# Windowed attention with sinks and top-128 experts: the first K and Q loaded uncast in halves, turned by fp32 products, later loads held by marks

## The chip, the cores and the metric

The kernel runs on one core of a Trainium2 chip. The core has TensorE (PE, with its weight loads shown apart as PEld), VectorE (DVE), ScalarE (ACT), GpSimd (POOL) and SyncE (SP), which issues most of the loads and stores. The metric is the device time of one execution in microseconds, as the median of several. A profiled execution gives a trace in which every instruction has its start and its length.

## The reference

Attention for 4 batches of 8 heads over 768 tokens of 64 columns. A query sees the 128 keys up to itself and the first 4 keys, the sinks. The result, laid out as rows of 512, goes through a block that picks the 128 rows with the largest gate score in each batch and adds the gated output of two layers to them.

```python
scores = scale * np.matmul(q, k.transpose(0, 1, 3, 2))
keep = is_sink | in_window          # 4 sinks, or 0 <= query - key < 128
scores = np.where(keep, scores, -1000000000.0)
a = softmax(scores); out = np.matmul(a, v)
x = out.transpose(0, 2, 1, 3).reshape(B, S, H * D)
scores = x @ w_gate
for b in range(B):                  # the 128 rows with the largest scores
    xe = x[b, top_idx]
    ye = np.maximum(xe @ w1, 0.0) @ w2
    out[b, top_idx] = xe + sigmoid(scores[b, top_idx])[:, None] * ye
```

## The kernel before

The work is cut into 24 steps: 4 batches, two groups of 4 heads each (a pair of heads shares the 128 rows of a tile, so a group is called a pair of tiles, K and Q), and three pairs of 128-token blocks. The order of instructions on each engine is the order in which the program writes them. Each engine takes its own in order and waits by semaphores for what others make.

A pair (b, g) needs K and Q turned, with the 64 columns of a head on the partitions. `transposes` (L210) turns them on TensorE in two halves of 6 products each into a PSUM bank, and ACT (`L228`) and DVE (`L230`) copy the banks to `KT` and `QT`. The bf16 input of later pairs comes from `plain_qk` (L105), which loads fp32 through SP into a buffer of the pool `raw` (three buffers), and `cast_qk` (L113), which casts it on POOL in two pieces for each tensor. The first pair alone goes another way: `load_qk` (L96) lets the DMA cast, which POOL issues (L103), and both halves are turned one head at a time, 24 products for a tensor (L221).

`scores` (L235) makes the score products of one step (L246), adds the masks (L256) and the sinks' scores (L263, L267) and lets ACT take the exponentials (L274; L276 and L277 in the last step of a pair). `values` (L279) multiplies them with V in fp32 (L295), once for each half `t` of the heads; DVE divides (L298, L299) into the rows `x`. V stands in three tiles: `vb` as loaded, and `vlo` and `vhi`, in which one half of the partitions holds V again and four of the others the sinks' V. POOL copies V into them (`copy_half_values` L134, `copy_half_heads` L138). For the first pair the sinks' V is loaded into the first block (L145) and spread over the six blocks by POOL (L149). All other pairs get it from a table `vst`, which DVE spreads out of `vsk` in `stage_sinks` (L196 to L202) and SP copies into place (`load_sink_values`, L129).

The prologue (L152 to L194) writes out loads, clearings and masks; then `fill` (L545) keeps TensorE at work with products of a unit matrix whose results nobody reads, the first pair is turned, and the scores of step 0 are made (L553 to L561). The loop (L593 on) makes values of step n, scores of the step two ahead, and the turning of the next pair, and SP's loads are put where the table `PAIRS_AT` (L580) says. `sp_after` (L589) is a mark: SP copies one element of a finished row to a scrap tile, so that it waits for that step before it goes on to the loads behind it.

Of the kernel before, what the change touches and what calls it, by code (L numbers as in the profile page):

```python
# [9 lines left out]
FP32 = mybir.dt.float32  # L10
BF16 = mybir.dt.bfloat16
# [19 lines left out]
def kernel(  # L31
# [41 lines left out]
    vlo = [const([128, 4, NB, VW], FP32, f"vlo{i}") for i in range(2)]  # L73
    vhi = [const([128, 4, NB, VW], FP32, f"vhi{i}") for i in range(2)]
    vsk = mp.tile([NSINK * B, H, D], FP32, name="vsk", tag="junk")
    vst = const([NSINK * B, H, NB, VW], FP32, "vst")
    ksk = [const([128, 2, 64], BF16, f"ksk{i}") for i in range(2)]
    ident_f = const([128, 128], FP32, "ident_f")
# [12 lines left out]
    smark = const([1, 24], FP32, "smark")  # L91
    part = const([128, 2], FP32, "part")

    QKF, QK, KT, QT, PT, X, SCOL = {}, {}, {}, {}, {}, {}, {}

    def load_qk(b, g, ts=(0, 1)):  # L96
        for t in ts:
            name = ("kb", "qb")[t]
            dst = stg.tile([128, 2, CT, D], BF16, name=name, tag=name)
            QK[(b, g, t)] = dst  # L100
            src = (k, q)[t][b, 4 * g:4 * g + 4, :, :].rearrange("(l e) (p c) d -> (e p) l (c d)", e=2, c=CT)
            for l in range(2):
                POOL.dma_start(out=dst[:, l, :, :].rearrange("p c d -> p (c d)"), in_=src[:, l, :])  # L103

    def plain_qk(b, g, ts=(0, 1)):  # L105
        for t in ts:
            dst = raw.tile([128, 2, CT * D], FP32, name="raw", tag="raw")
            QKF[(b, g, t)] = dst
            src = (k, q)[t][b, 4 * g:4 * g + 4, :, :].rearrange("(l e) (p c) d -> (e p) l (c d)", e=2, c=CT)
            for l in range(2):  # L110
                SP.dma_start(out=dst[:, l, :], in_=src[:, l, :])

    def cast_qk(b, g, t):  # L113
        name = ("kb", "qb")[t]
        dst = stg.tile([128, CT, 2, D], BF16, name=name, tag=name)
        QK[(b, g, t)] = dst
        src = QKF[(b, g, t)][:, :, :].rearrange("p l (c d) -> p c l d", c=CT)
        for c in (0, CT // 2):
            POOL.tensor_copy(out=dst[:, c:c + CT // 2, :, :], in_=src[:, c:c + CT // 2, :, :])  # L119
# [23 lines left out]
    def first_sink_values():  # L143
        for dst, r in ((vlo, 64), (vhi, 0)):
            SP.dma_start(out=dst[0][r:r + NSINK, :, 0, 0:D], in_=v[0, 0:4, 0:NSINK, :].rearrange("h s d -> s h d"))  # L145

    def spread_first_sinks(c0, c1):
        for dst, r in ((vlo, 64), (vhi, 0)):
            POOL.tensor_copy(out=dst[0][r:r + NSINK, :, c0:c1, 0:D],  # L149
                             in_=dst[0][r:r + NSINK, :, 0:1, 0:D].to_broadcast((NSINK, 4, c1 - c0, D)))  # L150

    for b in range(B):  # L152
        ACTE.dma_start(out=vsk[NSINK * b:NSINK * b + NSINK, :, :], in_=v[b, :, 0:NSINK, :].rearrange("h s d -> s h d"))
    DVE.memset(ones_b[:], 1.0)
    ACTE.activation(out=warm[:], in_=ones_b[:], func=ACT.Exp)
    POOL.memset(ident_f[:], 0.0)
    POOL.affine_select(out=ident_f[:], in_=ident_f[:], compare_op=ALU.not_equal, fill=1.0, base=0,
                       pattern=[[-1, 128]], channel_multiplier=1)
    DVE.tensor_copy(out=ident_b[:], in_=ident_f[:])
    load_qk(0, 0)  # L160
    for dst, r in ((vlo, 64), (vhi, 0)):
        DVE.memset(dst[0][r:r + 64, :, :, :], 0.0)
        DVE.memset(dst[0][r:r + NSINK, :, :, D:VW], 1.0)
    load_v_block(0, 0, 0)
    load_v_block(0, 0, 1)
    first_sink_values()
    for c in range(2, NB):
        load_v_block(0, 0, c)
    plain_qk(0, 1)
    for h in (4, 6):  # L170
        load_v_heads(0, h)
# [13 lines left out]
    spread_first_sinks(1, 2)  # L185
# [7 lines left out]
    DVE.memset(vlo[1][64:128, :, :, :], 0.0)  # L193
    DVE.memset(vhi[1][0:64, :, :, :], 0.0)  # L194

    def stage_sinks():  # L196
        DVE.memset(vst[:, :, :, D:VW], 1.0)
        DVE.memset(vb[1][:, :, :, D:VW], 1.0)
        for g in range(2):
            DVE.tensor_copy(out=vst[:, 4 * g:4 * g + 4, :, 0:D],  # L200
                            in_=vsk[:, 4 * g:4 * g + 4, :].unsqueeze(2).to_broadcast((NSINK * B, 4, NB, D)))
        load_sink_values(0, 1)  # L202

    def late_consts2():
        for c in range(NB):
            DVE.memset(sel[:, c, 1:2], float(128 * c))
        DVE.tensor_copy(out=iota_b[:], in_=iota_i[:])
        DVE.tensor_copy(out=sel[:, :, 0:1], in_=tok_i[:, :].unsqueeze(1).to_broadcast((128, NB, 1)))

    def transposes(b, g, t, halves=(0, 1)):  # L210
        if 0 in halves:
            (KT, QT)[t][(b, g)] = tp.tile([128, 2, S], BF16, name=("KT", "QT")[t], tag=("KT", "QT")[t])
        src = QK[(b, g, t)]
        dst = (KT, QT)[t][(b, g)]
        for half in halves:
            trp = bank("w", [128, CT // 2, 128], BF16, "trp")
            for i in range(CT // 2):
                c = half * (CT // 2) + i
                if (b, g) == (0, 0):
                    for l in range(2):  # L220
                        PE.transpose(out=trp[64 * l:64 * l + 64, i, :], in_=src[:, l, c, :], identity=ident_b[:])  # L221
                else:
                    PE.transpose(out=trp[:, i, :], in_=src[:, c, :, :].rearrange("p l d -> p (l d)"),  # L223
                                 identity=ident_b[:])
            o = dst[:, :, :].rearrange("d e (p c) -> d e p c", c=CT)[:, :, :, half * (CT // 2):(half + 1) * (CT // 2)]
            i = trp[:, :, :].rearrange("d c (e p) -> d e p c", e=2)
            if (half if (b, g) == (0, 0) else 0) == t:
                ACTE.copy(out=o, in_=i)  # L228
            else:
                DVE.tensor_copy(out=o, in_=i)  # L230
# [314 lines left out]
    def fill(count):  # L545
        z = bank("xg", [128, 4, 128], FP32, "z")
        for _ in range(count):
            PE.matmul(out=z[:, :, :], lhsT=ident_b[:, :], rhs=ident_b[:, :].unsqueeze(1).to_broadcast((128, 4, 128)),
                      start=True, stop=True, skip_group_check=True)
# [12 lines left out]

    WF = {}

# [28 lines left out]
    for n, (b, g, jp) in enumerate(steps):  # L593
# [157 lines left out]
```

## Time and profile before

| what | us |
|---|---|
| median of 3 runs (138.97 to 141.78) | 139.62 |
| the profiled execution | 138.69 |
| its span, first to last instruction | 136.8 |
| PE busy in the span | 114.3 |
| PEld busy | 94.0 |
| DVE busy | 97.9 |
| POOL busy | 77.5 |
| ACT busy | 70.7 |

The core moved 33.29 MB in the span, 243 GB/s on the average. A row of the timeline gives start, length, engine, line and operation, the tile written and the tiles read, the count of instructions that were merged, and in brackets the idle time of the engine just before and what ended it. A row of the stretches gives the stretch, its length, the busy time and the count of each engine, the clock granted to TensorE as a share of full speed, the mean share of the 16 DMA engines that were busy (it can go over 1, since times of packets overlap) and the rate. A row of the groups gives a line's busy time and the mean time of one instruction in ns.

### The profile page before, as it was taken

What the parts mean: (1) busy time and instruction counts of PE and PEld (TensorE: products, weight loads), DVE (VectorE), ACT (ScalarE), POOL (GpSimd) and SP (SyncE); (2) the same over time, 40 slices, a digit from 0 to 9 for tenths busy, and PEclk for the clock granted to TensorE, in tenths of its full rate; (3) what the DMA queues carried; (4) which work ended last, traced back from release to release, by engine and by line L of the source; (5) the groups of instructions that cost most, each with busy time, mean ns of one, the idle gap of its engine ahead of it and who ended that gap; (6) DMA issues with size and microseconds to landing.
All of it is one profiled execution on the core that took longest, in us unless ns stands there. A gap on an engine that the chain in (4) does not pass through costs nothing. (4 is left out here: it accounts for less than half of the span.)

```text
span 136.8 us, 6228 instructions
## 1 busy us (share of the span) xinstructions
PE 114.3 (84%) x2690; PEld 94.0 (69%) x2692; DVE 97.9 (72%) x293; ACT 70.7 (52%) x120; POOL 77.5 (57%) x100
## 2 busy tenths in 40 slices
PE   5977749689996889899979996988899999799750
PEld 2344629677895779797868885978777984586740
DVE  4779501935594969999598999968858657999540
ACT  3126760257757727675774764576384685043300
POOL 7719999945455963546089494852886530220520
PEclk9999995999999999999999999999999999999999
DMA  4999999937998976699999999699899384819131
GB/s 81 160 222 298 299 238 343 304 131 218 327 219 187 317 227 208 169 320 308 235 300 306 320 288 366 173 293 371 316 353 326 116 301 150 320 53 337 26 132 77
DMA packets 36622, 33.29 MB, mean 243 GB/s; under 512 B 26428, under 2 KB 26940, under 8 KB 36596
## 3 DMA queue, kind: packets, MB, share of 16 engines
q1 hardware_dynamic: 35236, 29.99, 74.3%
q0 software_dynamic: 1216, 2.88, 8.0%
q8 instruction: 21, 0.34, 1.1%
q10 hardware_dynamic: 144, 0.03, 0.1%
q14 instruction: 5, 0.04, 0.1%
HBM read 24.42 MB, written 8.91 MB: 244 GB/s over the span
## 5 line engine op out<-in xcount | busy, mean ns | idle before, releaser
L295 PE MATMUL xg<-vb,pt 128*64 128x65 f32 x704 | 50.2, 227 | 0.3 <-DVE x L299 0.3
L295 PE MATMUL xg<-vlo,pt 128*64 128x65 f32 x384 | 45.6, 226 | 3.0 <-issue 2.3
L295 PEld LDWEIGHTS xg<-vb,pt 128*64 128x64 f32 x704 | 45.3, 141 | 2.5 <-PE se L430 0.4
L295 PE MATMUL xg<-vhi,pt 128*64 128x65 f32 x320 | 41.9, 230 | 2.3 <-issue 2.3
L295 PEld LDWEIGHTS xg<-vlo,pt 128*64 128x64 f32 x384 | 36.8, 141 | 6.4 <-issue 5.0
L274 ACT ACTIVATE pt<-sc 128x1024 f32<-128x1024 f32 x32 | 31.0, 1021 | 14.7 <-PE sc L267 14.5
L295 PEld LDWEIGHTS xg<-vhi,pt 128*64 128x64 f32 x320 | 32.1, 141 | 0.6 <-issue 0.6
L299 DVE TENSOR_TENSOR x<-xg,rz 128x256 f32<-128x256 f32 x48 | 20.4, 425 | 1.8
L228 ACT COPY KT<-trp 128x768 bf16<-128x768 bf16 x15 | 12.2, 813 | 15.1 <-PE trp L223 10.7
L140 POOL COPY vlo<-vb 64x780 f32<-64x780 f32 x14 | 12.1, 863 | 13.4 <-DMA vb<-in_v_dram 8.3
L298 DVE RECIPROCAL rz<-xg 128x4 f32<-128x4 f32 x48 | 8.5, 177 | 15.6 <-PE xg L295 15.3
L315 DVE CUSTOM_DVE_ANT_0 junk<-x,wgb 128x512 f32<-128x512 f32 (+1 forms) x24 | 19.5, 814 | 0.1
L119 POOL CAST qb<-raw 128x768 bf16<-128x768 f32 x14 | 11.6, 857 | 7.7 <-DMA raw<-in_q_dram 7.7
L230 DVE COPY QT<-trp 128x768 bf16<-128x768 bf16 x15 | 14.2, 949 | 0.9 <-PE trp L221 0.5
L140 POOL COPY vhi<-vb 64x780 f32<-64x780 f32 x14 | 13.1, 937 | 2.5 <-DMA xe<-out_dram,idx 1.8
L246 PE MATMUL sc<-QT,KT 64*64 64x192 bf16 (+2 forms) x384 | 12.6, 242 | 2.3 <-ACT pt L274 1.4
L575 POOL CAST w_sb<-wf 128x1024 bf16<-128x1024 f32 x8 | 8.3, 1038 | 8.7 <-DMA wf<-in_moe_w_dram 8.7
L378 DVE TENSOR_SCALAR_CACHE_REDUCE G<-sbc,scol 128x768 bf16<-128x768 f32 (+5 forms) x18 | 11.0, 677 | 2.9 <-ACT sbc L364 2.9
L119 POOL CAST kb<-raw 128x768 bf16<-128x768 f32 x14 | 11.6, 854 | 0.4
L246 PEld LDWEIGHTS <-KT 64*64 64x64 bf16 x384 | 7.7, 106 | 5.5 <-issue 3.4
L512 POOL DMA_INDIRECT out_dram<-yo,idx x4 | 3.9, 980 | 11.5 <-DVE x L299 5.1
L256 PE MATMUL sc<-mask_b,ident_b 64*64 64x256 bf16 x192 | 10.1, 269 | 0.1
(122 smaller groups left out, 200.8 us busy)
## 6 DMA issues: line engine op xcount, KB each, us to landing
out_dram<-x SPq DMA_DIRECT2D x24, 256.0 KB
raw<-in_k_dram SPq DMA_DIRECT2D x14, 384.0 KB
raw<-in_q_dram SPq DMA_DIRECT2D x14, 384.0 KB
vb<-in_v_dram SPq DMA_DIRECT2D x14, 384.0 KB
wf<-in_moe_w_dram SPq DMA_DIRECT2D x8, 512.0 KB
rows<-x SPq DMA_DIRECT2D x6, 256.0 KB
vb<-in_v_dram SPq DMA_DIRECT2D x6, 128.0 KB
kb<-in_k_dram POOLq DMA_DIRECT2D x2, 192.0 KB, 5.3
```

The source lines that it names most:

```text
L119: POOL.tensor_copy(out=dst[:, c:c + CT // 2, :, :], in_=src[:, c:c + CT // 2, :, :])
L140: POOL.tensor_copy(out=dst[h // 4][r:r + 64, h % 4:h % 4 + 2, :, :].rearrange("p h c d -> p (h c d)"), in_=vb[b % 2][r:r + 64, h:h + 2, :, ...
L228: ACTE.copy(out=o, in_=i)
L230: DVE.tensor_copy(out=o, in_=i)
L246: PE.matmul(out=sc[e][h:h + 64, l, r, h:h + nq], lhsT=kt[rows, e, kc * 128 + h:kc * 128 + h + 64], rhs=qt[rows, e, kc * 128 + h:kc * 128 + ...
L256: PE.matmul(out=sc[e][h:h + 64, l, :, :].rearrange("p r (w n) -> p r w n", w=2)[:, :, :, h:h + 64], lhsT=ident_b[rows, 64 * l:64 * l + 64] ...
L274: ACTE.activation(out=pt[:, e, :, :, :], in_=sc[e][:, :, :, :], func=ACT.Exp, scale=0.125)
L295: PE.matmul(out=xg[64 * m:64 * m + 64, i, l, :], lhsT=p, rhs=w, start=(i == 0 and l == 0 and n < 2), stop=(i == 1 and l == 1 and n >= len( ...
L298: DVE.reciprocal(out=rz[:, :, :, :], in_=xg[:, :, :, D:VW])
L299: DVE.tensor_tensor(out=X[b][:, 2 * jp:2 * jp + 2, 256 * g:256 * g + 256].rearrange("p j (l e d) -> p j l e d", l=2, e=2)[:, :, :, t, :], ...
L315: DVE.tensor_tensor_reduce(out=junk[:, c0:c1], in0=X[b][:, j, c0:c1], in1=wgb[:, c0:c1], scale=1.0, scalar=start, op0=ALU.mult, op1=ALU.ad ...
L378: DVE.tensor_scalar(out=self.G[c][:, a:hi], in0=self.sbc[:, a:hi], scalar1=SCOL[self.b][:, c:c + 1], scalar2=0.0, op0=ALU.is_gt, op1=ALU.a ...
```

## The change

- The first pair's K and Q are loaded as fp32 into two buffers of `raw`, by halves of the tokens (384 each) and by halves of the partitions: K by SP, the first half of Q by ACT, the second halves by SP (`load_first`). No casting load is left.
- `first_transposes` turns them by plain fp32 products with the fp32 unit matrix, 12 products for a half of a tensor in two banks of three, one copied by ACT and one by DVE. The first halves are turned before the scores of step 0, the second halves inside step 0, between its two values products.
- The scores of step 1 stand behind step 0's values, those of step 2 inside step 1, and the first turning of the second pair behind them.
- The fills are 7, 1, 2 and 3 products in place of 13, 3, 2 and 3.
- The first sinks' V is loaded by ACT into a tile `sst` and spread by DVE for `vhi` and by POOL for `vlo`. `vsk` is loaded by POOL in place of ACT, behind the first copies of V.
- `mark` makes SP wait for a landed load: for the fourth and the sixth block of V ahead of K and Q of the second pair, and for that K and that Q ahead of the last two V loads of the second pair.
- DVE clears `vlo[0]` ahead of the cast of `ident_b`; `clear_halves` clears the tiles of the second pair after the first turning. `stage_sinks` and its copies by SP come at the end of step 0, and K and Q of the third pair are loaded in step 1 in place of step 0.

```diff
+    def load_first(t, half, queue, es=(0, 1)):
+        src = (k, q)[t][0, 0:4, 384 * half:384 * half + 384, :].rearrange("(l e) (p c) d -> e p l (c d)", e=2, c=HT)
+        for e in es:
+            queue.dma_start(out=FIRST[t][64 * e:64 * e + 64, half, :, :], in_=src[e])
...
+    def mark(i, src):
+        SP.dma_start(out=smark[:, 24 + i:25 + i], in_=src)
...
+    def spread_first_sinks(dst, r, engine):
+        engine.tensor_copy(out=dst[0][r:r + NSINK, :, :, 0:D],
+                           in_=sst[r:r + NSINK, :, :].unsqueeze(2).to_broadcast((NSINK, 4, NB, D)))
+
+    load_first(0, 0, SP)
+    load_first(1, 0, ACTE, (0,))
+    load_first_sinks()
+    load_first(1, 0, ACTE, (1,))
...
-    DVE.tensor_copy(out=ident_b[:], in_=ident_f[:])
-    load_qk(0, 0)
...
+    DVE.memset(vlo[0][64:128, :, :, :], 0.0)
+    DVE.memset(vlo[0][64:64 + NSINK, :, :, D:VW], 1.0)
+    DVE.tensor_copy(out=ident_b[:], in_=ident_f[:])
+    DVE.memset(vhi[0][0:64, :, :, :], 0.0)
+    DVE.memset(vhi[0][0:NSINK, :, :, D:VW], 1.0)
+    spread_first_sinks(vhi, 0, DVE)
...
+    load_first(0, 1, SP)
+    load_first(1, 1, SP)
+    for c in range(2, NB):
+        load_v_block(0, 0, c)
...
+    spread_first_sinks(vlo, 64, POOL)
     copy_half_values(0, 0, 0, 2)
-    spread_first_sinks(2, NB)
+    for b in range(B):
+        POOL.dma_start(out=vsk[NSINK * b:NSINK * b + NSINK, :, :], in_=v[b, :, 0:NSINK, :].rearrange("h s d -> s h d"))
+    mark(0, vb[0][0:1, 0, 3, 0:1])
+    plain_qk(0, 1, (0,))
+    mark(1, vb[0][0:1, 0, 5, 0:1])
+    plain_qk(0, 1, (1,))
     copy_half_values(0, 0, 2, NB)
     cast_qk(0, 1, 0)
     cast_qk(0, 1, 1)
+    mark(2, QKF[(0, 1, 0)][0:1, 1, 0:1])
+    load_v_heads(0, 4)
+    mark(3, QKF[(0, 1, 1)][0:1, 1, 0:1])
+    load_v_heads(0, 6)
...
+    def first_transposes(t, half, kind):
+        if half == 0:
+            (KT, QT)[t][(0, 0)] = tp.tile([128, 2, S], BF16, name=("KT", "QT")[t], tag=("KT", "QT")[t])
+        src = FIRST[t][:, half, :, :].rearrange("p l (c d) -> p l c d", c=HT)
+        dst = (KT, QT)[t][(0, 0)][:, :, 384 * half:384 * half + 384].rearrange("d e (p c) -> d e p c", c=HT)
+        for part in range(2):
+            trp = bank(kind, [128, 3, 128], FP32, "trf")
+            for i in range(3):
+                for l in range(2):
+                    PE.matmul(out=trp[64 * l:64 * l + 64, i, :], lhsT=src[:, l, 3 * part + i, :], rhs=ident_f[:, :],
+                              start=True, stop=True)
+            o, i = dst[:, :, :, 3 * part:3 * part + 3], trp[:, :, :].rearrange("d c (e p) -> d e p c", e=2)
+            if part == t:
+                ACTE.copy(out=o, in_=i)
+            else:
+                DVE.tensor_copy(out=o, in_=i)
...
-    fill(13)
-    transposes(0, 0, 0)
-    fill(3)
+    fill(7)
+    first_transposes(0, 0, "w")
     sink_keys(0, 0)
-    transposes(0, 0, 1)
-    fill(2)
+    fill(1, "sc")
+    first_transposes(1, 0, "xg")
+    clear_halves()
+    fill(2, "sc")
     scores(0, 0, 0)
-    fill(3)
-    stage_sinks()
+    fill(3, "w")
...
-    PAIRS_AT = {0: ((2, 0), (2, 1)), 2: ((3, 0),), 3: ((3, 1),)}
+    PAIRS_AT = {1: ((2, 0), (2, 1)), 2: ((3, 0),), 3: ((3, 1),)}
...
-        ahead = [] if n == 1 else [n + 2]
+        ahead = [1] if n == 0 else [] if n == 1 else [n + 2]
...
-        if turn == 0:
+        if turn == 0 and n > 1:
             transposes(nxt[0], nxt[1], 0, (0,))
...
-        if n in (0, 2):
+        if n == 0:
+            first_transposes(0, 1, "w")
+            first_transposes(1, 1, "sc")
+        if n in (1, 2):
             scores(*steps[n + 1])
+        if n == 1:
+            transposes(nxt[0], nxt[1], 0, (0,))
...
+        if n == 0:
+            stage_sinks()
+            load_sink_values(0, 1)
```

More of the change, by code (lines that the diff above doesn't have):

```diff
@@ L75 @@
     vsk = mp.tile([NSINK * B, H, D], FP32, name="vsk", tag="junk")
+    sst = mp.tile([128, 4, D], FP32, name="sst", tag="hT")
     vst = const([NSINK * B, H, NB, VW], FP32, "vst")
@@ L90 @@
     tok_i = const([128, 1], I32, "tok_i")
-    smark = const([1, 24], FP32, "smark")
+    smark = const([1, 32], FP32, "smark")
     part = const([128, 2], FP32, "part")
     QKF, QK, KT, QT, PT, X, SCOL = {}, {}, {}, {}, {}, {}, {}
[L96 to L103, printed above, removed]
+    HT = CT // 2
+    FIRST = [raw.tile([128, 2, 2, HT * D], FP32, name="raw", tag="raw") for _ in range(2)]
+    def load_first(t, half, queue, es=(0, 1)):
+        src = (k, q)[t][0, 0:4, 384 * half:384 * half + 384, :].rearrange("(l e) (p c) d -> e p l (c d)", e=2, c=HT)
+        for e in es:
+            queue.dma_start(out=FIRST[t][64 * e:64 * e + 64, half, :, :], in_=src[e])
     def plain_qk(b, g, ts=(0, 1)):
@@ L141, in copy_half_heads, with load_first_sinks @@
                              in_=vb[b % 2][r:r + 64, h:h + 2, :, :].rearrange("p h c d -> p (h c d)"))
[L143 to L153, printed above, removed]
+    def mark(i, src):
+        SP.dma_start(out=smark[:, 24 + i:25 + i], in_=src)
+    def load_first_sinks():
+        for r in (64, 0):
+            ACTE.dma_start(out=sst[r:r + NSINK, :, :], in_=v[0, 0:4, 0:NSINK, :].rearrange("h s d -> s h d"))
+    def spread_first_sinks(dst, r, engine):
[5 more added lines that the diff above has]
+    load_first(1, 0, ACTE, (1,))
     DVE.memset(ones_b[:], 1.0)
@@ L184 @@
     POOL.tensor_copy(out=mask_b[:], in_=mask_f[:])
-    spread_first_sinks(1, 2)
+    spread_first_sinks(vlo, 64, POOL)
     copy_half_values(0, 0, 0, 2)
-    spread_first_sinks(2, NB)
+    for b in range(B):
[4 more added lines that the diff above has]
+    plain_qk(0, 1, (1,))
     copy_half_values(0, 0, 2, NB)
@@ L190, with clear_halves @@
     cast_qk(0, 1, 1)
+    mark(2, QKF[(0, 1, 0)][0:1, 1, 0:1])
+    load_v_heads(0, 4)
+    mark(3, QKF[(0, 1, 1)][0:1, 1, 0:1])
+    load_v_heads(0, 6)
     POOL.iota(iota_i[:], pattern=[[1, 128]], base=0, channel_multiplier=0)
     POOL.iota(tok_i[:], pattern=[[0, 1]], base=0, channel_multiplier=1)
-    DVE.memset(vlo[1][64:128, :, :, :], 0.0)
-    DVE.memset(vhi[1][0:64, :, :, :], 0.0)
+    def clear_halves():
+        DVE.memset(vlo[1][64:128, :, :, :], 0.0)
+        DVE.memset(vhi[1][0:64, :, :, :], 0.0)
     def stage_sinks():
         DVE.memset(vst[:, :, :, D:VW], 1.0)
-        DVE.memset(vb[1][:, :, :, D:VW], 1.0)
-        for g in range(2):
+        for g in (1, 0):
             DVE.tensor_copy(out=vst[:, 4 * g:4 * g + 4, :, 0:D],
                             in_=vsk[:, 4 * g:4 * g + 4, :].unsqueeze(2).to_broadcast((NSINK * B, 4, NB, D)))
-        load_sink_values(0, 1)
     def late_consts2():
+        DVE.memset(vb[1][:, :, :, D:VW], 1.0)
         for c in range(NB):
@@ L218, in transposes @@
                 c = half * (CT // 2) + i
[L219 to L224, printed above, removed]
+                PE.transpose(out=trp[:, i, :], in_=src[:, c, :, :].rearrange("p l d -> p (l d)"), identity=ident_b[:])
             o = dst[:, :, :].rearrange("d e (p c) -> d e p c", c=CT)[:, :, :, half * (CT // 2):(half + 1) * (CT // 2)]
             i = trp[:, :, :].rearrange("d c (e p) -> d e p c", e=2)
-            if (half if (b, g) == (0, 0) else 0) == t:
+            if t == 0:
                 ACTE.copy(out=o, in_=i)
@@ L543, in down, with fill @@
                           start=(fc == 0), stop=(fc == 7))
-    def fill(count):
-        z = bank("xg", [128, 4, 128], FP32, "z")
+    def fill(count, kind="xg"):
+        z = bank(kind, [128, 4, 128], FP32, "z")
         for _ in range(count):
```

9 lines of the change are left out of this document (removed).

## The prediction

> **What bounds the kernel now.** I read the busy time of the engines by stretches first, cut at two places that the timeline of TensorE gave me: the first score products (11.48 us) and the scores of the fourth step (27.43 us).
>
> ```profile
> span 136.8 us, 6228 instructions
> 0.00:11.48 11.48, 8.69 (x66) 3.84 (x67) 8.08 (x16) 3.30 (x5) 7.04 (x22) 1.00 0.85 165
> 11.48:27.43 15.95, 11.47 (x267) 9.74 (x267) 7.91 (x21) 7.11 (x11) 15.45 (x19) 0.89 1.08 299
> 27.43:129.10 101.67, 91.60 (x2334) 78.66 (x2336) 80.28 (x255) 59.67 (x103) 53.14 (x59) 1.00 0.84 254
> ```
>
> After length come PE, weight loads, DVE, ACT and POOL, then granted clock, DMA share and GB/s. From 27.43 to 129.10 PE is busy 90% of the time: what is won ahead of 27.43 moves the rest forward, unless a load is then late. The change edits only what lies ahead of that point. There 11.48 us pass before any score, and 15.95 us hold 11.47 us of PE work, part of it slow. The timeline of PE shows where:
>
> ```profile
> 1.64 5.34 PE L548 MATMUL z<-ident_b 128*128 128x512 bf16 x13 [1.64 <-DVE ident_b L159]
> 7.64 0.86 PE L221 MATMUL trp<-ident_b,kb 128*64 128x128 bf16 x23 [0.49 <-DMA kb<-in_k_dram]
> 8.43 0.82 PE L548 MATMUL z<-ident_b 128*128 128x512 bf16 x3
> 9.73 0.86 PE L221 MATMUL trp<-ident_b,qb 128*64 128x128 bf16 x23 [0.30 <-DMA qb<-in_q_dram]
> 11.48 0.52 PE L246 MATMUL sc<-QT,KT 64*64 64x192 bf16 x16 [0.36 <-ACT QT L228]
> 13.46 0.24 PE L295 MATMUL xg<-vlo,pt 128*64 128x65 f32 x1 [0.37 <-issue]
> 14.31 0.52 PE L246 MATMUL sc<-QT,KT 64*64 64x192 bf16 x16
> 14.66 0.39 PE L256 MATMUL sc<-mask_b,ident_b 64*64 64x256 bf16 x8
> 15.09 0.27 PE L295 MATMUL xg<-vlo,pt 128*64 128x65 f32 x1
> 18.14 0.51 PE L223 MATMUL trp<-ident_b,kb 128*128 128x128 bf16 x6 [0.34 <-POOL kb L119]
> 20.76 0.27 PE L295 MATMUL xg<-vhi,pt 128*64 128x65 f32 x1 [1.85 <-issue]
> 23.92 0.51 PE L223 MATMUL trp<-ident_b,qb 128*128 128x128 bf16 x6
> ```
>
> Columns: start, time, instruction, count, idle time before it and its releaser. Both turnings wait for the casting loads; then comes a hole of 1.85 us in the middle of a values product, put down to nothing the profile shows. The stretches around it (the third of values products alone), and the DMA queues from 17.9 to 20.8 us:
>
> ```profile
> 16.00:20.00 4.00, 1.75 (x43) 1.25 (x42) 0.61 (x2) 3.31 (x7) 3.89 (x6) 1.00 1.23 231
> 20.00:24.00 4.00, 3.24 (x63) 3.17 (x63) 0.61 (x2) 0.14 (x1) 3.88 (x7) 0.57 0.97 347
> 21.00:23.40 2.40, 2.40 (x49) 2.40 (x48) 0.50 0.99 352
> q8 instruction: 1, 0.02, 2.7%
> ```
>
> The same view of 0 to 17.9 us has no q8 line, so this is the first instruction packet, and it lies just ahead of the hole. I read the hole as PE out of instructions, its packet stuck behind the loads that SP had queued. After those thin 4 us the clock falls to 0.57 for the next 4, and a values record takes 49 ns there.
>
> **Part 1, to the first scores.** K and Q no longer go through casting loads, whose time to landing and whose cost on POOL's queue were
>
> ```profile
> 1.48 1.32 POOL L103 DMA_DIRECT2D kb<-in_k_dram  x2 [0.16 <-issue]
> 2.75 1.11 POOL L103 DMA_DIRECT2D qb<-in_q_dram  x2
> DMA to landing us min/median/max: 5.2/5.3/5.4
> ```
>
> (the last for K). Now SP and ACT each load a half of 393 KB from 0.75 us. At 347 GB/s (20 to 24 us) both halves take 2.3 us, at the opening's 165 GB/s 4.8; with some 1.2 us to the first byte, an estimate from these rows is landing between 4.2 and 6.7 us. That is not what PE waits for, since DVE now clears a tile ahead of the cast of ident_b:
>
> ```profile
> 0.83 0.06 DVE L154 MEMSET ones_b<- 128x1 bf16 x1 [0.83 <-PEq L732]
> 1.35 0.23 DVE L159 CAST ident_b<-ident_f 128x128 bf16<-128x128 f32 x1 [0.47 <-POOL ident_f L157]
> 1.96 1.36 DVE L162 MEMSET vlo<- 64x1560 f32 x1 [0.38 <-issue]
> 3.40 0.08 DVE L163 MEMSET vlo<- 4x24 f32 x1
> ```
>
> ident_b: 0.89 + 0.38 + 1.36 + 0.16 (gap and small clearing) + 0.23 = 3.0, so fills start at 3.1, not 1.64. Seven at 5.34/13 = 0.41 end at 6.0. Then the fp32 products, which have no row. Nearest are the fp32 values products, here those between 26 and 27 us, and the copies that bracket 384 fp32 columns:
>
> ```profile
> 26.00:27.00 1.00, 0.98 (x32) 0.98 (x32) 1.00 1.13 311
> L364 ACT COPY sbc<-bc 128x512 f32<-128x512 f32 x3 | 1.8, 592 | 4.9 <-PE bc L362 4.9
> L364 ACT COPY sbc<-bc 128x256 f32<-128x256 f32 x3 | 1.1, 376 | 0.0
> ```
>
> Each fp32 product there is two records (704 of them for 352 products), 31 ns each at 65 columns. Half a tensor is 12 products, 24 records. If the columns set the pace, 128 of them take 60 ns and a half 1.45 us; if the load of 64 weights does, 31 ns and 0.73 us. I take 1.45, because the 16 score records with 64 weights each go by in 0.35 us (14.31 to 14.66), 22 ns each: weights alone hardly need 31. The clock was still low in the 13 fills (0.41 each) and up in the three at 8.43 (0.27 each); I charge 0.25 for a part at half rate. K done 7.7, one fill 0.2, Q done 9.35, its last copy 0.48 (between the two copies) and handovers 0.15: first scores at 10.0, a gain of 1.5. Q's fp32 halves are needed at 7.9, which covers the loads above.
>
> DVE and POOL each wait for the loaded sinks before spreading them. Behind DVE's spread stand the copies of K; behind POOL's the vlo/vhi copies.
>
> ```profile
> 5.23 0.26 SPq L145 DMA_DIRECT2D vhi<-in_v_dram  x1
> 10.05 0.40 POOL L149 COPY vhi<-vhi 4x256 f32<-4x256 f32 x1 [0.59 <-DMA vhi<-in_v_dram]
> 10.40 0.61 POOL L136 COPY vlo<-vb 64x520 f32<-64x520 f32 x1
> 11.63 1.77 POOL L149 COPY vlo<-vlo 4x1024 f32<-4x1024 f32 x1
> 15.06 1.04 POOL L136 COPY vlo<-vb 64x1040 f32<-64x1040 f32 x1
> L200 DVE COPY vst<-vsk 16x1536 f32<-16x1536 f32 x2 | 2.9, 1502 | 0.0
> ```
>
> Before, a sink load needed up to 4.8 us. Issued by 2.0 it is there by 6.8, DVE's 1.5 us of spreading ends by 8.3, just when K's copy is wanted: 0 to 0.3, I take 0. POOL, rid of 2.43 us of load issue, spreads for 1.77 x 1.5 = 2.7 us, from 4.5 or at worst 6.8, and two copies of 0.61 end at 8.4 or 10.7; values are due at 12.0.
>
> **Part 2, first scores to fourth-step scores.** From the rows: scores to first values 1.98; values 0.85; then, new here, the second halves of K and Q, 2.90 (bounds 1.46 and 2.90, twice that at half clock); values again 0.85; the second scores, now without values behind them, expose the exponential: 1.98 until the next values, of which some 1.1 idle. Those take 0.98 plus handover, 1.0; third scores 0.8; turning K 0.4; values 1.0; and from turning Q to the fourth scores 27.43 - 23.92 = 3.51. Sum 15.27 against 15.95. Against the 15.95 the added 2.90 and the exposed wait are paid by the hole (1.85), by the half-rate stretch (2.7 us from 20.76 at 49 ns a record instead of 31: 1.0), and by waits for ACT and POOL around 16 to 18 us. The whole: 1.48 + 0.68 = 2.2 us sooner at that point.
>
> Why the hole should go: the four marks on SP hold K, Q and the last two V loads of the second pair until earlier ones land, and Q's load waits for a raw buffer until K's products are done (about 14.3). Instructions fetched from 12 us on then find at most one pair-load ahead, 786 KB or 2.3 us at 347 GB/s, and the PE needs them at about 17.
>
> [...]
>
> **Part 3, what moves behind.** On SP the marks, then the copy of vst, stand ahead of the third pair's loads:
>
> ```profile
> 14.24 2.39 SPq L131 DMA_DIRECT2D vlo<-vst  x1
> 17.31 1.14 SPq L111 DMA_DIRECT2D raw<-in_k_dram  x2
> 24.14 1.59 POOL L119 CAST kb<-raw 128x768 bf16<-128x768 f32 x2
> 30.90 0.51 PE L223 MATMUL trp<-ident_b,kb 128*128 128x128 bf16 x6
> ```
>
> vst is now built after the first step's values (about 17) in 2 x 1.5 us, so SP passes it at 20.1, issues two sink copies (the second took 0.68 between these rows), a mark and the gate's load (2.2 in all, an estimate from that row), and K of the third pair at 22.3, not 17.3. Landed by about 25.5 (3.2 us, with 786 KB at 300 GB/s), cast by 27.1; PE wants it at 30.90 - 2.2 = 28.7. The slack was 5.2 and is 1.6: no cost, but this is the cover that could go. POOL's four sink-table loads stand ahead of its later copies (2.43 for four, as the casting loads took); two copies of 1.04 behind them end near 13, values want them at 17. Later loads follow marks tied to the steps, and shift with them.
>
> The profiled execution took 138.69 us, 1.9 more than its span; the median is 139.62. Less 2.2: 136.5 and **137.4**.
>
> **Rivals.** *Cheap products*: at 31 ns a record, 1.45 us less before the scores and 1.45 after, of which I keep 2.1 since fills, copies and waits then show: 135.3. For: nothing but that weight and column rates can't be told apart at 65 columns.
> *The hole stays*, with its slow stretch (1.85 + 1.0): 2.2 - 2.85, so 140.3. For: the same count of instructions falls at the same products (fills take 16 rows out, turning 96 rows become 192, and 76 rows of the third scores and of one turning now come later: 4 more); against: less is queued, and the exposed wait there gives it cover.
> *Half clock* (the slower side): PE starts 1.5 us later, does half the fills, and has holes for copies and exponentials between products. If the clock has not risen by the end of the first step's products, all 48 products cost double: 4 x 1.45 = 5.8, less the 0.25 counted, 143.0. It decides from about two halves at half rate (2.7, no gain left to speak of). For: the fall to 0.57 after 1.75 of 4 us busy; against: PE is busy nearly without break from 3.1 to 9.4, as it was from 1.64 to 6.98 before. [...]
> *Given back later*: the third pair is late by 2 us or more beyond its slack: 139.4. For: DMA would idle near 20 us; against: the slack.
> *The marks do nothing*, since buffers hold the same loads: the time is the forecast's.
>
> **Numbers.** Forecast with or without the marks' part 0.47 (its own range 136.2 to 138.8), cheap products 0.15, hole 0.15, half clock 0.13, given back 0.10. The range runs from 135.0 (cheap products) to 141.3 (past the hole's case; half clock is left out). Two per cent, 2.8 us, is about what a measurement of this kernel tells from no change. Faster by more: cheap products and a third of the forecast, 0.32; slower by more: half clock and the tail of the hole, 0.16; within 0.52.
>
> **What would show it.** First scores near 10.0 and the fp32 rows at 60 ns; no long "issue" gap between 16 and 21 us and a granted clock of 1.00 there; third-pair casts on POOL ending before PE turns them; the fourth step's scores near 25.3. Wrong if PE's first scores come at 11 or later, if the clock is low in the products, or if the gain at the fourth step is gone at 40 us.

## The result and the profile after

The changed kernel takes 146.73 us (median of 4 runs, 146.01 to 148.61) where the kernel before took 140.34 beside it (138.97 to 141.78, 4 runs): a ratio of 1.048, with an interval of 1.038 to 1.059. It is slower by 5%. The profiled execution took 147.36 us, its span 145.4. All ratios compare only the fast runs of each kernel, those within 1.5% of its fastest, and where a table gives none, none is on record.

First the stretches of the changed kernel, cut at the same two points as before the change, the first scores and the scores of the fourth step; then stretches of 4 us. Columns as in the prediction.

```profile
0.00:11.46 11.46, 8.13 (x58) 4.92 (x59) 6.70 (x13) 2.86 (x5) 7.34 (x20) 1.00 0.91 183
11.46:26.12 14.66, 12.88 (x315) 11.01 (x315) 9.93 (x26) 8.31 (x13) 8.09 (x12) 1.00 0.78 195
26.12:137.60 111.48, 96.19 (x2345) 82.43 (x2343) 79.54 (x255) 59.94 (x104) 59.97 (x66) 0.97 0.84 255
...
24.00:28.00 4.00, 3.78 (x108) 3.32 (x107) 2.43 (x13) 1.92 (x4) 2.98 (x4) 1.00 0.74 167
28.00:32.00 4.00, 1.11 (x35) 0.77 (x32) 0.61 (x2) 2.86 (x4) 0.55 (x2) 1.00 0.98 351
32.00:36.00 4.00, 3.32 (x54) 3.12 (x54) 0.61 (x2) 0.81 (x1) 3.35 (x5) 0.58 1.13 315
```

The part ahead of the fourth step did gain: its scores start at 26.12 instead of 27.43. Right behind that point lies the damage. From 28 to 32 us TensorE is busy for 1.11 of 4 us, and for the 4 us after that its clock is 0.58. The timeline of the changed kernel, several engines together, shows what was missing:

```profile
19.20 0.94 DVE L213 COPY vst<-vsk 16x1536 f32<-16x1536 f32 x1
21.22 0.57 SPq L144 DMA_DIRECT2D smark<-raw  x1
21.85 0.38 SPq L126 DMA_DIRECT2D vb<-in_v_dram  x1
22.28 0.66 SPq L131 DMA_DIRECT2D vlo<-vst  x1
22.99 0.61 SPq L131 DMA_DIRECT2D vhi<-vst  x1
23.64 0.59 SPq L616 DMA_DIRECT2D smark<-x  x1
24.27 0.38 SPq L689 DMA_DIRECT2D wgb<-in_moe_w_gate_dram  x1
24.76 0.88 SPq L111 DMA_DIRECT2D raw<-in_k_dram  x2
25.74 1.06 SPq L111 DMA_DIRECT2D raw<-in_q_dram  x2
...
31.80 1.60 POOL L119 CAST kb<-raw 128x768 bf16<-128x768 f32 x2 [3.45 <-DMA raw<-in_k_dram]
32.68 0.82 PE L249 MATMUL trp<-ident_b,kb 128*128 128x128 bf16 x6 [3.02 <-POOL kb L119]
```

Read it from the bottom: TensorE idled 3.02 us for POOL's cast of the third pair's K; POOL had idled 3.45 us for that K to land; SP had issued it at 24.76. In the kernel before SP issued it at 17.31. The sinks' table `vst` was ready at 20.1; SP came to its copy at 22.28, behind the last of the four marks (21.22).

To follow where time comes and goes later, I take the first division of each step (the reciprocal on VectorE that ends the first half of its values) as a milestone. In step 3, the kernel before, then the changed one:

```profile
32.31 0.18 DVE L298 RECIPROCAL rz<-xg 128x4 f32<-128x4 f32 x1 [2.22 <-PE xg L295]
```

```profile
35.05 0.18 DVE L323 RECIPROCAL rz<-xg 128x4 f32<-128x4 f32 x1 [6.28 <-PE xg L320]
```

| first division of step | 0 | 1 | 2 | 3 | 6 | 9 | 12 | 15 | 18 | 21 | end of span |
|---|---|---|---|---|---|---|---|---|---|---|---|
| after less before, us | 0.0 | -1.8 | -1.1 | +2.7 | +3.4 | +2.4 | +5.7 | +4.6 | +8.6 | +7.7 | +8.6 |

So there are two losses: 3.8 us between steps 2 and 3, and some 6 us in jumps much later (steps 10 to 12, 16 to 18), where the program is the same as before. The first comes again in a second profile of both kernels and the second hardly does, as the last part of the experiments shows. The experiments take them in turn.

### The profile page after: what moved, and what is told of

It reads as the page before. It is cut to its first block, busy times and chain, and to the rows that moved or that the text cites. A ratio compares the mean times of both kernels' runs of the same rounds, so it can differ in the third digit from the quotient of the medians.

```text
span 145.4 us, 6323 instructions
## 1 busy us (share of the span) xinstructions
PE 119.3 (82%) x2732; PEld 99.8 (69%) x2732; DVE 97.8 (67%) x296; ACT 71.7 (49%) x122; POOL 76.6 (53%) x97
## 5 line engine op out<-in xcount | busy, mean ns | idle before, releaser
L320 PE MATMUL xg<-vb,pt 128*64 128x65 f32 x704 | 52.4, 231 | 2.9 <-issue 2.7
L320 PEld LDWEIGHTS xg<-vb,pt 128*64 128x64 f32 x704 | 46.8, 144 | 6.9 <-issue 4.7
L320 PE MATMUL xg<-vlo,pt 128*64 128x65 f32 x384 | 46.8, 230 | 3.4 <-issue 2.3
L320 PE MATMUL xg<-vhi,pt 128*64 128x65 f32 x320 | 42.8, 232 | 0.0
L320 PEld LDWEIGHTS xg<-vlo,pt 128*64 128x64 f32 x384 | 37.9, 145 | 4.1 <-issue 3.2
L119 POOL CAST qb<-raw 128x768 bf16<-128x768 f32 x14 | 12.7, 934 | 10.9 <-DMA raw<-in_q_dram 10.9
L340 DVE CUSTOM_DVE_ANT_0 junk<-x,wgb 128x512 f32<-128x512 f32 (+1 forms) x24 | 18.2, 756 | 0.1
L255 DVE COPY QT<-trp 128x768 bf16<-128x768 bf16 x14 | 13.3, 948 | 0.2 <-PE trp L249 0.2
L249 PE MATMUL trp<-ident_b,kb 128*128 128x128 bf16 x84 | 7.3, 225 | 4.7 <-POOL kb L119 3.0
L301 ACT ACTIVATE pt<-sc 128x512 f32<-128x512 f32 x16 | 9.6, 601 | 1.2 <-PE sc L292 1.0
```

Source lines behind the costliest of these rows:

```text
L301: ACTE.activation(out=pt[:, e, :, 0, :], in_=sc[e][:, :, 0, :], func=ACT.Exp, scale=0.125)
L320: PE.matmul(out=xg[64 * m:64 * m + 64, i, l, :], lhsT=p, rhs=w, start=(i == 0 and l == 0 and n < 2), stop=(i == 1 and l == 1 and n >= len( ...
L340: DVE.tensor_tensor_reduce(out=junk[:, c0:c1], in0=X[b][:, j, c0:c1], in1=wgb[:, c0:c1], scale=1.0, scalar=start, op0=ALU.mult, op1=ALU.ad ...
```

## The experiments

| run | median us (range, runs) | before, same chip | ratio (95%) |
|---|---|---|---|
| e1 third pair early | 146.83 (143.47 to 148.62, 4) | 140.70 | |
| e2 no marks | 145.61 (142.85 to 147.97, 5) | 140.70 | 1.046 (1.017 to 1.074) |
| e3 before, 84 more rows | 138.91 (135.52 to 143.33, 10) | 140.70 | 0.982 (0.972 to 0.992) |
| e4 unit matrix first | 148.65 (148.26 to 149.13, 4) | 140.70 | 1.069 (1.052 to 1.085) |
| e5 after, 172 more rows | 147.12 (144.90 to 148.70, 4) | 142.48 | 1.040 (1.012 to 1.069) |
| e6 before, 128 more rows | 141.53 (140.16 to 144.52, 4) | 142.48 | 1.008 (0.991 to 1.025) |
| e7 third pair early, no marks | 144.33 (142.58 to 145.12, 4) | 142.48 | 1.023 (0.996 to 1.050) |
| e8 after, 128 more rows | 148.99 (145.59 to 154.72, 4) | 142.48 | |
| e9 as e7, 172 more rows | 140.82 (139.71 to 143.09, 4) | 138.41 | 1.021 (1.000 to 1.041) |
| e10 as e7, 42 more rows | 144.99 (142.93 to 146.40, 4) | 138.41 | |
| e11 before with 84 rows, third pair late | 139.29 (136.72 to 140.88, 4) | 138.41 | |
| e16 as e3, timed again | 140.10 (136.69 to 143.98, 12) | 140.51 | 0.996 (0.989 to 1.003) |
| e17 changed start at its best | 144.00 (141.51 to 147.89, 6) | 140.51 | 1.021 (1.006 to 1.037) |

### The late third pair: e1, e2, e7, e11

e1 issues the third pair's loads in step 0 again, ahead of the sink copies and the gate's load:

```diff
-    PAIRS_AT = {1: ((2, 0), (2, 1)), 2: ((3, 0),), 3: ((3, 1),)}
+    PAIRS_AT = {0: ((2, 0), (2, 1)), 2: ((3, 0),), 3: ((3, 1),)}
...
             stage_sinks()
-            load_sink_values(0, 1)
...
             plain_qk(i // 2, i % 2, (t,))
+        if n == 0:
+            load_sink_values(0, 1)
```

> The changed kernel with K and Q of the third pair loaded in step 0 again, ahead of the sink copies that wait for vst and of the gate's load; marks stay. Theory (the third pair comes too late): K's casts end some 4 us sooner, the hole of 3.0 us before its turning and the half-rate stretch behind it go, so 4 us of the 6.4 come back: 142.5. If the later losses too are only a consequence of that lateness, all comes back and 1 more: 139. Rival (the loss lies elsewhere, in fetching of instructions): 146 to 147.

e2 takes the four marks out and leaves the rest:

```diff
-    mark(0, vb[0][0:1, 0, 3, 0:1])
-    mark(1, vb[0][0:1, 0, 5, 0:1])
-    mark(2, QKF[(0, 1, 0)][0:1, 1, 0:1])
-    mark(3, QKF[(0, 1, 1)][0:1, 1, 0:1])
```

> The changed kernel without its four marks on SP. Theory (the marks leave the DMA engines without work from 13 to 14, 20 to 21 and 22.5 us, and so delay the third pair): the third pair's K is issued 1 to 2 us sooner, 1 to 2 us come back: 145. Rival (the marks keep the instruction packets from queuing): a hole comes near 17 to 20 us and it is slower, 148 to 150. If neither matters: 146 to 147.

e7 does both edits.

> The changed kernel without its four marks and with the third pair's loads issued a step earlier: everything that holds loads back is gone, the new first pair stays. Theory 'loads': 138 to 141.5 us, and under 96 us from the end of step 2 to the end of the last step. Theory 'boundaries' (same rows as the changed kernel, so the same boundaries): 143.5 to 147 us, with holes of 1.4 us or more again near 62 to 70 us.

The timelines at the third pair's K and at the idle time of TensorE nearest to it, of e1, e2 and e7 in this order:

```profile
22.23 1.50 SPq L111 DMA_DIRECT2D raw<-in_k_dram  x2
28.37 1.59 POOL L119 CAST kb<-raw 128x768 bf16<-128x768 f32 x2 [0.76 <-DMA raw<-in_k_dram]
31.49 0.22 PE L320 MATMUL xg<-vlo,pt 128*64 128x65 f32 x1 [1.45 <-DMA vlo<-vst]
32.74 0.18 DVE L323 RECIPROCAL rz<-xg 128x4 f32<-128x4 f32 x1 [4.02 <-PE xg L320]
```

```profile
22.63 1.97 SPq L111 DMA_DIRECT2D raw<-in_k_dram  x2
28.32 1.59 POOL L119 CAST kb<-raw 128x768 bf16<-128x768 f32 x2 [2.93 <-DMA raw<-in_k_dram]
31.08 0.22 PE L316 MATMUL xg<-vlo,pt 128*64 128x65 f32 x1 [1.07 <-issue]
32.04 0.18 DVE L319 RECIPROCAL rz<-xg 128x4 f32<-128x4 f32 x1 [3.35 <-PE xg L316]
```

```profile
19.60 1.97 SPq L111 DMA_DIRECT2D raw<-in_k_dram  x2
26.82 1.59 POOL L119 CAST kb<-raw 128x768 bf16<-128x768 f32 x2 [0.35 <-DMA raw<-in_k_dram]
29.36 0.51 PE L245 MATMUL trp<-ident_b,kb 128*128 128x128 bf16 x6
31.00 0.18 DVE L319 RECIPROCAL rz<-xg 128x4 f32<-128x4 f32 x1 [2.45 <-PE xg L316]
```

Each edit alone brings the K over two us forward and ends the wait for its cast. But both still idle in the next values. In e1 the view names the sink copies, which now stand behind the pair; they had landed by 31.0, though, and what then held TensorE to 31.49 is an instruction block that begins just there (the part on holes), as it is in e2's 1.07 us. The clock is at half from 32.0 to 35.4 in e1. Only with both edits is the place clear: step 3's division comes at 31.00 instead of 35.05, and the clock stays up until 89.9. A second profile of e7's kernel (e14, below) has 31.01, a second one of the changed kernel 34.90. So late loads, and the half clock behind their wait, cost 4.0 us by step 3 (3.9 in the second profiles). In time e7 stands at 1.023 where the changed kernel stands at 1.048, but its interval (0.996 to 1.050) takes in both. That is not the whole loss: e7 missed the 141.5 us of "loads" by 3, and the figures of "boundaries" held for it (144.33 us, holes of 1.75 and 1.43 us at 62.0 and 67.5). By the medians alone e1 (146.83) would be the rival's case, and e2 (145.61) lies between its figures.

e11 tries the same thing on the other side, with the start of the kernel before:

```diff
-    PAIRS_AT = {0: ((2, 0), (2, 1)), 2: ((3, 0),), 3: ((3, 1),)}
+    PAIRS_AT = {2: ((2, 0), (2, 1), (3, 0)), 3: ((3, 1),)}
```

> The kernel before with 84 more rows (138.9 us), and of the change one thing alone: K and Q of the third pair issued later, in step 2 behind its mark, instead of in step 0. If a late third pair is what the changed kernel pays for: TensorE waits 1.5 to 4 us for its cast ahead of the turning near 26 to 30 us, the clock falls to half for 3.4 us behind that wait, and the time is 141.5 to 144.5 us. If the slack covers it: 138 to 140 us, no wait there over 0.6 us.

Its timeline at that place:

```profile
20.49 0.88 SPq L111 DMA_DIRECT2D raw<-in_k_dram  x2
24.93 1.59 POOL L119 CAST kb<-raw 128x768 bf16<-128x768 f32 x2 [1.83 <-DMA raw<-in_k_dram]
26.76 0.51 PE L223 MATMUL trp<-ident_b,kb 128*128 128x128 bf16 x6
```

K went out 3.95 us later than in e3 (16.54) and was still in time, so the slack covers that much in this kernel, where the cast came 4.4 us after the issue and not 7.0: a step's delay alone did no harm. In the changed kernel the marks, the sink copies and the gate's load stood ahead of the pair when it went out at 24.76.

### The start: e4, e9, e17

e4 casts the unit matrix ahead of DVE's clearing and makes 11 fills:

```diff
+    DVE.tensor_copy(out=ident_b[:], in_=ident_f[:])
     DVE.memset(vlo[0][64:128, :, :, :], 0.0)
     DVE.memset(vlo[0][64:64 + NSINK, :, :, D:VW], 1.0)
-    DVE.tensor_copy(out=ident_b[:], in_=ident_f[:])
...
-    fill(7)
+    fill(11)
```

> The changed kernel with ident_b cast ahead of the clearing of vlo, and 11 fills in place of 7. Theory for the start (the first products ran at half rate because PE began at 3.2 us): K's first products 1.5 us long in place of 2.7, first scores near 10.2 in place of 11.46. If the third pair bounds the rest, the time does not change (146 to 147) and its hole grows by 1.2; if it does not, 145.3.

K's products took 1.53 us as expected, but TensorE waited 0.97 us for K's load ahead of them, and first scores came at 10.99 instead of 11.46 (10.2 expected). The third pair was waited for again (2.68 us). The total rose to 148.65, above every figure given for it, with 9.4 us of the holes that the next part is about.

e9 is e7 with 93 products of 32 x 38 in place of 7 fills (its expectation is in the next part). The starts of the changed kernel and of e9 on TensorE:

```profile
3.19 3.17 PE L573 MATMUL z<-ident_b 128*128 128x512 bf16 x7 [3.19 <-DVE ident_b L167]
6.29 2.71 PE L232 MATMUL trf<-ident_f,raw 128*64 128x128 f32 x24
9.25 1.53 PE L232 MATMUL trf<-ident_f,raw 128*64 128x128 f32 x24
11.46 0.53 PE L271 MATMUL sc<-QT,KT 64*64 64x192 bf16 x16
...
14.21 2.82 PE L232 MATMUL trf<-ident_f,raw 128*64 128x128 f32 x48
```

```profile
3.19 3.13 PE L576 MATMUL z<-ident_b 128*32 128x38 bf16 x93 [3.19 <-DVE ident_b L167]
6.25 1.53 PE L228 MATMUL trf<-ident_f,raw 128*64 128x128 f32 x24
8.04 1.53 PE L228 MATMUL trf<-ident_f,raw 128*64 128x128 f32 x24
10.25 0.53 PE L267 MATMUL sc<-QT,KT 64*64 64x192 bf16 x16
```

Both begin at 3.19. In e9 the clock came up at 6.2, K's 24 records took 1.53 us and the scores began at 10.25; in the changed kernel it came up at 8.7, K's records took 2.71 us and the scores began at 11.46. All three starts with 71 or 93 small products in place of the fills (e5, e8, e9) have it up at 6.2 to 6.5, the other seven that begin at 3.2 at 7.9 to 9.2; no run shows why.

e17 joins what helped: e7 with e4's cast and, in place of the fills, 136 such small products.

> The changed start at its best: no marks, third pair early, the unit matrix cast ahead of the clearing, 136 small warm-up products in place of 7. If the new first pair is worth its price once nothing comes late and the clock is up in time: first scores at 9.5 to 10.3 us, step 2 ended by 24 to 24.7 us, and a time of 0.975 to 0.995 of the kernel before. If the second halves' products inside step 0 cost more than the start gains: step 2 ended at 25 us or later than in the kernel before with 84 more rows by 1.5 us, and a ratio of 1.00 to 1.03.

First scores came at 10.39, but step 2's division only at 26.44 (24 to 24.7 expected; e9 has 25.00), and the time is 1.021 of the kernel before (1.006 to 1.037): with the third pair in time and the clock up early, the new first pair still wins nothing, as the expectation's second case had it. Against e3, e17 divides in step 0 0.9 us sooner (13.37 against 14.24). From there to step 1 it takes 6.4 us against 4.95, with the 2.82 us of the second halves in it, and on to step 2 6.7 against 4.1 (e9: 5.4). In that last stretch TensorE waited 0.43 us for the second pair's Q, 0.60 for a copy of QT and 0.62 at an instruction block. That the second halves take back what the start gives fits these figures; no run takes them out alone.

### Holes at instruction blocks: e3, e6, e5, e8, e9, e10

The hole that the prediction read as a late instruction packet can be placed exactly. Counted over the weight loads, products, semaphore and drain rows of TensorE, 449 records stand ahead of it. In the 19 traces of this study 96 idle times of 0.75 us and more have 449 or 450 plus a multiple of 256 records ahead of them, and each of these ends 1.2 to 1.6 us after the end of an instruction packet. For 94 of them the view names no releaser ("issue"); for one in e1 and one in e10 it names a load and ACT. All other idle times of that length have another engine or a load as their releaser. I read this as a program that comes to TensorE in blocks of 256 records, so that TensorE stands when the next block comes late; the traces show the spacing and the packets, not how they are fetched. One such idle time in the changed kernel:

```profile
67.92 0.52 PE L271 MATMUL sc<-QT,KT 64*64 64x192 bf16 x13
70.97 0.27 PE L271 MATMUL sc<-QT,KT 64*64 64x192 bf16 x3 [2.53 <-issue]
```

The change adds some 84 records (the traces hold 5509 against 5423), and so moves every boundary against the work. If that were the later loss, other row counts should take it away. Warm-up products add the rows, with the columns of the fills shared among them; first e3, then e5 and e9, the others by the counts in their expectations:

```diff
-    fill(13)
+    z = bank("xg", [128, 4, 128], FP32, "z")
+    for _ in range(55):
+        PE.matmul(out=z[:, 0, 0:120], lhsT=ident_b[:, :], rhs=ident_b[:, 0:120], start=True, stop=True,
+                  skip_group_check=True)
```

```diff
-    fill(7)
+    z = bank("xg", [128, 4, 128], FP32, "z")
+    for _ in range(93):
+        PE.matmul(out=z[0:32, 0, 0:38], lhsT=ident_b[:, 0:32], rhs=ident_b[:, 0:38], start=True, stop=True,
+                  skip_group_check=True)
```

> The kernel before with 55 fill products of 120 columns in place of 13 of 512: the same columns, 84 more rows of products and weights ahead of everything, which is what the change adds, and nothing else. Theory (the later losses come from where the instruction blocks begin): holes after 40 us at other places, 2 to 4 us slower than before: 142 to 144. Rival (the loss comes from the loads only): as before, 139.5 to 140.8.

> The kernel before with 128 more TensorE rows (77 warm-up products of 86 columns in place of 13 of 512): boundaries half a block away from where they were. Theory 'boundaries': anywhere from 138 to 147 us, off the kernel before by over 2 us one way or the other, with holes over 1.4 us if it is slower. Theory 'loads': 138.5 to 141 us, no hole over 1.4 us behind the third step.

> The changed kernel with 93 small warm-up products in place of 7 large ones, which adds 172 TensorE rows; with the 84 that the change adds this makes 256, one whole block of fetched instructions, so from the first step on the block boundaries fall on the same work as in the kernel before. Theory 'boundaries' (the time lost from the third step to the end, 102.8 us against 93.9 before, comes from fetch holes at boundaries that fall badly): 140 to 142.5 us, with under 96 us from the end of step 2 to the end of the last step. Theory 'loads' (the later holes come from loads that run later against the work, wherever the boundaries lie): 145 to 149 us, and that stretch stays at 100 us or more.

> The changed kernel with 128 more TensorE rows (71 warm-up products of 50 columns in place of 7 of 512): boundaries half a block away. Theory 'boundaries': differs from the changed kernel's 146.7 by 2 us or more. Theory 'loads': 145 to 149 us.

> The changed kernel without marks, third pair early, and 172 more TensorE rows (93 small warm-up products in place of 7), so that the block boundaries fall on the work as in the kernel before. If what is left of the loss without late loads (144.3 us, 1.023 of the kernel before) is the place of the boundaries: 138 to 141 us, and about 104 to 106 us from the end of step 3 to the end. If it belongs to the new first pair wherever the boundaries lie: 143 to 145.5 us, and 109 us or more for that stretch.

> The same kernel with 42 more rows in place of 172 (28 warm-up products of 128 columns): boundaries as in the kernel before with 128 more rows, which took 141.5 us. If boundaries decide the rest: 140 to 143 us with holes at like places as there. If the new first pair does: 143 to 145.5 us, as with no rows added.

In e3 the early hole, the half clock behind it and 4 us were gone by step 2, with nothing of the change in it; at 138.91 it was faster than either of its theories said. e6 missed both of its own: 1.008 of the kernel before, yet with holes of 1.65 and 2.08 us. The later loss did not go by boundaries either: the changed kernel took 147 to 149 us at three row counts, its wait for the third pair came in all (4.37 us in e5, 3.9 in e8), and behind step 3 they need much the same (next table). The 2.3 us by which e8 differs rest on runs from 145.6 to 154.7 us and decide nothing. Of e9 and e10, one fits the time given for boundaries (140.8) and one does not (145.0). But the kernel before was faster on their chip (138.41), so that e9 stands at 1.021 of it, as e7 does at 1.023; and the profiles of e9 and e10 are 2.0 us apart at step 3 already, with the clock up at 6.2 and 9.2, and 0.7 behind it.

### Is it chance? e12 to e16

Four kernels were profiled a second time on one chip, unchanged: the kernel before (142.06 us), e3 (143.48), e7 (144.49) and the changed kernel (145.57).

> The kernel before, profiled once more. Idle time of TensorE at block boundaries behind the end of step 3 was 4.0 us in its first profile and 4.2 to 6.6 in the three kernels with its start and other row counts. If holes are smaller with this start: 3 to 6.5 us again. If it is chance from execution to execution: it may come out at 7 to 9.

> The kernel before with 84 more rows, profiled once more (4.2 us of such holes in its first profile, which at 135.5 us was its fastest run). Smaller with this start: 3 to 6.5 us. Chance: 7 to 9.

> The changed kernel without marks and with the third pair early, profiled once more, with the same rows as the one before it (7.3 us of such holes). Larger with the changed start: 6.5 to 9.5 us, and 104 us from the end of step 3. Chance: 3 to 6, and 100 to 102 us.

> The changed kernel, profiled once more (7.3 us of such holes; third pair's K cast waited for 3.0 us, half clock behind it). The wait for K and the half clock behind it come again, 2.5 to 3.5 us and 3.4 us, whatever the holes do. Larger with the changed start: holes of 6.5 to 9.5 us. Chance: 3 to 6.

> The kernel before with 84 more TensorE rows, timed on another chip. If the row count alone takes the early hole and its half clock away and nothing gives it back: a ratio to the kernel before of 0.96 to 0.985. If holes further back eat the gain, as in its second profile: 0.985 to 1.01.

The sums below take idle times over 0.25 us at such records, behind step 3's first division:

| kernel | step 3's division at, us | from there to the end of the span | of it holes |
|---|---|---|---|
| before, two profiles | 32.31, 32.28 | 104.5, 107.9 | 3.7, 9.1 |
| e3, e13, e16 (84 more rows) | 28.28, 30.51, 30.19 | 105.4, 111.1, 104.6 | 4.2, 8.3, 2.6 |
| e6, e11 | 29.80, 28.16 | 108.5, 109.3 | 7.4, 6.4 |
| after, two profiles | 35.05, 34.90 | 110.3, 108.7 | 7.3, 7.0 |
| e7, e14 | 31.00, 31.01 | 110.7, 111.3 | 7.3, 10.4 |
| e1, e2, e4, e5, e8 | 32.74, 32.04, 33.67, 37.27, 36.95 | 112.6, 110.8, 112.5, 109.4, 109.7 | 10.3, 9.2, 9.4, 8.7, 8.4 |
| e9, e10, e17 | 29.79, 31.82, 31.21 | 108.3, 109.0, 111.8 | 7.6, 7.7, 8.6 |

The same program loses 3.7 us to holes in one execution and 9.1 in another, 4.2 and 8.3, 2.6. By the expectations e12 and e13 speak for chance, e14 and e15 for the changed start; in e15 the wait for K (2.90 us) and 3.4 us at half clock came again. The second profiles of the two kernels compared here, 107.9 and 108.7 us from step 3 on, differ by 0.8 us where the first differ by 5.8. Even e3's gain in time is of that kind. Its 4 us by step 2 come in all three profiles (23.3 to 23.5, against 27.3), but at the boundary behind 961 records it had no hole, and its second and third profile have one:

```profile
29.55 0.22 PE L295 MATMUL xg<-vlo,pt 128*64 128x65 f32 x1 [2.12 <-issue]
```

```profile
29.23 0.22 PE L295 MATMUL xg<-vlo,pt 128*64 128x65 f32 x1 [1.80 <-issue]
```

and e16, with 12 runs, found 0.996 (0.989 to 1.003) where e3 had found 0.982. What is left is a difference of means: 6.0 us of holes in seven profiles with the old start (2.6 to 9.1), 8.5 in twelve with the changed one (7.0 to 10.4), and 107.4 against 110.4 us from step 3 to the end. The ranges overlap, but the changed start never came below 7.0. It fits the rest of the loss (2.7 us by step 3, some 3 behind it, against 6.4 between the medians). That the start causes it is not shown. Why packets should come later for so long behind a changed start, where SP's order is the same again, was not found; no run isolates it.

## Why the prediction was wrong

A gain of 2.2 us was forecast and a loss of 6.4 measured. Of the 8.6 us between them 0.9 were missing at the fourth scores (1.3 sooner, not 2.2), 4.0 are the third pair, and the rest comes later.

**Part 1, the start: one term mis-sized.** Fills from 3.1 (3.19), seven of them, 60 ns a record at full clock (64 measured, 1.53 us for 24): all as reckoned, and the loads were there. The "0.25 for a part at half rate" was 1.18 (2.71 against 1.53), since the clock rose at 8.7 and not before K's products. First scores came at 11.46, not 10.0. e9, whose clock rose at 6.2, has 10.25, so the rest of the sum was right to 0.25. The prediction's own sign, "first scores at 11 or later", fired. In the runs whose first product starts at 3.2 us the clock rose at 6.2 (e9), 6.5 (e5), 8.0 (e7), 8.7 (the changed kernel) and 9.2 (e10), 3.0 to 6.0 us behind that product. The cost should have been a range, not a point.

**Part 2, first to fourth scores: the size right, the reason wrong.** 14.66 us against 15.27 forecast; the new products of the second halves took 2.82 for 2.90. The hole did go from 17 to 20 us. But "the four marks on SP hold K, Q and the last two V loads" was not needed for it: e2 has no marks and no hole there, and e3 loses the hole by a row count alone. So the credit of 2.85 us can be had from where a block boundary falls. Whether that alone paid it here is open: e5 and e9, which have a whole block more than the kernel before, have no hole at their first two boundaries either.

**Part 3, the third pair: the step that failed.** "The slack was 5.2 and is 1.6: no cost." SP issued K at 24.76, not 22.3: `vst` was ready at 20.1 as reckoned, but the marks let SP through to its copy only at 22.28. Then 786 KB were to land in 3.2 us; issue to cast took 7.0. The 3.2 is short by its own terms, since 786 KB at 300 GB/s take 2.6 us and Part 1 put 1.2 us ahead of the first byte (before, the first packet of SP's queue came at 1.87, 1.1 us behind the issue at 0.75). The trace of before had a better row: the same K, issued at 17.31, was all landed at 22.9 by its semaphore, 5.6 us later. I had divided one tensor by a high rate, where the profile above has 167 GB/s from 24 to 28 us. Q goes out a microsecond behind K and the gate's load just ahead; that they slow it is likely, but no run takes them away. In the three kernels shown with other places of that load issue to cast took 6.1, 5.7 and 7.2 us, in e11 4.4. In the place of 1.6 us of slack stood a wait of 3.02, and 3.4 us at half clock behind it.

**The rest, "what is won ahead of 27.43 moves the rest forward":** it did not, for the reason just given. Behind step 3 the holes differ from execution to execution by more than the gain that was forecast, and what part of the later loss is the change's stays open.

**Rivals.** *Given back later* named the mechanism and got 0.10 and 2 us; it was 4.0: a wait of 3.02, and a half clock next that it left out, though the profile of before showed one (0.57 behind the hole). *Half clock* cost 1.2 in the products, not 5.8. *Cheap products* is refuted by the 64 ns. *The marks do nothing* fits the hole, but they delay the third pair (24.76 against 22.63 in e2). *The hole stays* did not come true, yet it asked the right question, at which products the packets fall: I stopped at the first boundary instead of asking for all twenty. The 0.32 for "faster by more" is 0.31 by its own terms (0.15 and a third of 0.47).

## What to carry to other kernels

A load that is moved behind a mark has to be priced from its new issue to its landing with everything that is issued around it, by a row for a whole such group and not by size over the best rate (7.0 us from issue to cast here, where 3.2 had been reckoned). A wait on TensorE can be worth more than its length: the changed kernel's 3.02 us had 3.4 us at half clock behind it. A hole that belongs to an instruction block can go with an edit that only adds or removes rows (the 1.85 us that end at 20.76 in the kernel before are not there in e3), and can come back at another boundary (2.12 and 1.80 us in e3's second and third profile): it is no gain to credit to a change, and one profile of each kernel doesn't tell a difference in such holes.

## What the hardware showed that I had not expected

- Holes 256 records apart on TensorE: all 94 idle times of 0.75 us and more for which the view names no releaser lie behind 449 or 450 records plus a multiple of 256; they are up to 3.17 us long and end 1.2 to 1.6 us behind the packet.
- The sum of these holes varies within one program from 2.6 to 8.3 us (e3, e13, e16), whose runs spread from 135.5 to 144.0 us.
- Apart from the starts and the ends of the spans, the clock at half lasted 3.4 us, or 6.8 twice (e5, e8, behind waits of 4.4 and 3.9 us). It did not follow every hole: e9 had one of 2.5 us from 39.2 us on and kept its clock.
